# One planner for five engines: a planning delay for TensorE steps, other engines for the scaling of probabilities, and another way to turn q and k in two pairs

## The chip, the core and the metric

The kernel runs on one core of one Trainium2 chip. The core has TensorE (PE in the profile; its weight loads are the row PEld), VectorE (DVE), ScalarE (ACT) and GpSimd (POOL); SyncE (SP) issues all DMAs of this kernel. The metric is the device time of one execution in microseconds (us), median over several executions. One further execution was profiled.

## The reference

Three stages follow one another. Attention over 4 batches with 8 heads of 576 rows and 64 columns, a causal mask and a bias from a running sum; then an expert layer that takes the maximum of three products; then a second layer with a rational function.

```python
scores = scale * np.matmul(q, k.transpose(0, 1, 3, 2))
cum = np.cumsum(np.maximum(s, 0.0), axis=-1)
bias = -(cum[:, :, :, None] - cum[:, :, None, :])
scores = np.where(causal, -1000000000.0, scores + np.minimum(bias, 0.0))
attn = np.exp(scores - max);  attn = attn / (sum + 1e-09)
x = np.matmul(attn, v)                      # then 2304 tokens x 512
h = max(x @ w1, x @ w2, x @ w3);  x = h @ w_out          # d_ff 768
h = x @ w_in;  g = P(h) / Q(h);  out = g @ w_out2        # d_ff 2048
```

All products of float32 data are kept exact enough by splitting an operand into a rounded high part and the remaining low part, and adding three products.

## The kernel before, in words

**Attention.** The 32 heads are worked on in 16 pairs; pairs 0 to 3 are batch 0, and so on. For one pair:

- `load_qk` brings q and k into the tiles `raw_k` and `raw_q`. `prep_pe` (pairs 0 to 3, `pr < KM`, KM being 4) turns them by products with an identity matrix on TensorE (L401, 36 products of 64x64 in three steps: k, q and a rest `r`), copies the high part out of PSUM (L234) and subtracts for the low part on VectorE (L408). `prep` (the other pairs) turns them with VectorE's transpose instruction (L416, one for k and one for q), copies the high part on ScalarE or VectorE (L234) and subtracts on GpSimd or VectorE (L237). Its loads are eight DMAs of 140 KB in place of two of 288 KB.
- `scores` multiplies q by k and adds the bias (L450, four groups of row tiles), VectorE adds the mask and takes the row minimum (L467), ScalarE does exp and the row sum (L474).
- `norm` scales the rows by the reciprocal of their sum (L483 on GpSimd or VectorE, L481 on ScalarE), ten tiles for a pair: first tiles 2, 1, 0 of both heads, then tiles 4, 3. In pairs 0 to 3 the planner chooses between GpSimd, ScalarE and VectorE; in later pairs GpSimd does all ten.
- `flip` turns the scaled probabilities on TensorE (L515, 30 products in ten steps); ScalarE or VectorE copies them out (tile `PT`). `values` multiplies by v (L558); the result is split into `x` (L234, L570).

**First expert layer.** `experts` does one of 36 groups for a batch (12 products each, L186 with 288 columns). A group of a batch needs `x` of all four pairs of it, so TensorE has such groups to do only from the end of pair 3 on. The weights are loaded, decoded on VectorE (L594, L596, L598) and split. VectorE or ScalarE takes the result (`hs`, L674, L234).

**The rest.** When the last pair is done, its tiles are freed, and the weights of the second layer come back from DRAM (`ws`). TensorE does the remaining expert groups meanwhile, then `moe1_out`, and then the chunks of the second layer (L186 with 384 columns, L894), 96 of them.

**What sets the order.** Nothing is scheduled while the program runs: every engine works through its own list in order, and a waiting instruction holds up everything behind it. The lists come from `Plan.issue`, which runs once while the program is built. A step has engines that can do it with a cost in us on each, a rank (about the pair's number, plus a fraction for the stage), and the steps that it depends on. `est[m]` is the planned time at which step m's inputs are there: the planned end of the step before it plus a lag for the handover (`LAG`). Again and again the planner takes the step that can start first, and among those that could start on an engine at once the one of the lowest rank. A step that more than one engine could do (`anyof`) goes by planned end, weighted by `PRICE`. So a cost or a planned time that is changed alters no instruction by itself but the order on every engine, and through it the PSUM banks and the engine of the steps that have a choice.

Of the kernel before, what the change touches and what calls it, by code (L numbers as in the profile page):

```python
# [24 lines left out]
class Plan:  # L25
# [3 lines left out]

    LAG = {"pe": 0.2, "dve": 0.12, "act": 0.14, "pool": 0.09, "sp": 0.0, "ctl": 0.0}  # L30
    SAME = {"pe": 0.0, "dve": 0.11, "act": 0.1, "pool": 0.05, "sp": 0.0, "ctl": 0.0}
    BEGIN = {"dve": 0.9, "act": 2.0, "pool": 0.75, "sp": 0.75}
    AHEAD = 5.0
    TURN = 0.2
# [28 lines left out]
    def issue(self):  # L63
        steps = self.steps
        left = [len(s[3]) for s in steps]
        after = [[] for _ in steps]
        for n, s in enumerate(steps):
            for p in s[3]:
                after[p].append(n)
        end = [0.0] * len(steps)  # L70
        est = [0.0] * len(steps)
        engine = {e: self.BEGIN.get(e, 0.0) for s in steps for e in s[0]}
        ready = {e: set() for e in engine}
        for n, s in enumerate(steps):
            if not left[n]:
                for e in s[0]:
                    ready[e].add(n)
        idle = [(0.0, b) for b in self.banks]
        wire = 0.0
        mode = None  # L80
        for _ in steps:
            best = None
            for e, cand in ready.items():
                t = engine[e]
                mine = None
                for n in cand:
                    engs, rank, _, _, take, _, kb, new = steps[n]
                    start = max(t, est[n], wire - self.AHEAD if kb else 0.0)
                    if take:
                        if len(idle) < len(take):  # L90
                            continue
                        start = max(start, idle[len(take) - 1][0])
                    if len(engs) > 1 and any(max(engine[o], est[n]) + c * self.PRICE[o] < start + engs[e] * self.PRICE[e] for o, c in engs.items() if o != e):
                        continue
                    key = (max(start, t + 0.1), rank + (self.STAY if new and new != mode else 0.0), n)
                    if mine is None or key < mine[0]:
                        mine = (key, start)
                if mine is not None and (best is None or mine[1] < best[0]):
                    best = (mine[1], mine[0][2], e)
            start, n, e = best  # L100
            engs, _, fn, _, take, free, kb, new = steps[n]
            cost = engs[e]
            if new:
                cost += self.TURN if new != mode else 0.0
                mode = new
            for o in engs:
                ready[o].discard(n)
            for h in take:
                h.bank = idle.pop(0)[1]
            fn(e) if len(engs) > 1 else fn()  # L110
            engine[e] = start + cost
            if kb:
                wire = max(wire, start + cost) + kb / 190.0
                end[n] = wire + 2.0
            else:
                end[n] = start + cost
            lag = self.LAG[e]
            for h in free:
                idle.append((end[n] + lag, h.bank))
                idle.sort(key=lambda x: x[0])  # L120
            for m in after[n]:
                if "ctl" in steps[m][0]:
                    at = start
                else:
                    at = end[n] + (0.0 if kb else self.SAME[e] if list(steps[m][0]) == [e] else lag)
                est[m] = max(est[m], at)
                left[m] -= 1
                if not left[m]:
                    for o in steps[m][0]:
                        ready[o].add(m)  # L130
        return max(end)
# [3 lines left out]
def kernel(  # L135
# [25 lines left out]
    KM = DM // 128  # L161
# [32 lines left out]
    def open_pool(name, **kw):  # L194
        g = tc.tile_pool(name=name, bufs=1, reuse_waits="tile", **kw)
        open_pools[name] = g
        return g.__enter__()
# [29 lines left out]
    def anyof(engs, rank, fn, reads=(), writes=(), free=(), pre=()):  # L227

        if len(engs) == 1:
            return plan.add(engs, rank, lambda: fn(*engs), reads, writes, (), free, pre=pre)  # L230
        return plan.add(engs, rank, fn, reads, writes, (), free, pre=pre)
# [7 lines left out]
    def dm(rank, kb, out, in_, reads=(), writes=(), pre=()):  # L239
        return plan.add({"sp": 0.45}, rank, lambda: nc.sync.dma_start(  # L240
            out=out() if callable(out) else out, in_=in_() if callable(in_) else in_), reads, writes, kb=kb, pre=pre)
# [4 lines left out]
    at = open_pool("at", side="right")  # L246
# [30 lines left out]
    def smc(y, i):  # L277
        return SMC[i] + y * (3 if i < 3 else 2)
# [10 lines left out]
    def raw_of(pr, nm):  # L289

        return (RAW[pr][nm], ("x", 2 * pr - 2 + (nm == "q"))) if pr in (1, 2) else (raw[nm], ("raw", nm))
# [9 lines left out]
    def load_qk(pr, rank, pre=()):  # L301


        b, h = divmod(2 * pr, H)
        if pr < KM:
            for nm, src in (("k", k), ("q", q)):
                t, key = raw_of(pr, nm)
                dm(rank, 288, t[:, 0:S], src[b, h:h + 2].rearrange("y (p f) d -> (y p) (f d)", p=64),
                   [key], [("raw", pr, nm)], pre)
            return  # L310
        for nm, src in (("k", k), ("q", q)):
            t, key = raw_of(pr, nm)
            for y in range(2):
                x = src[b, h + y].rearrange("(p f) d -> p (f d)", p=32)
                for u in range(2):
                    dm(rank, 143, t[64 * y + 32 * u:64 * y + 32 * u + 32, 0:1120],
                       x[:, 32 * u:32 * u + 1120], [key], [("raw", pr, nm, y, u)], pre)

    def load_v(pr, rank, nj, last):
# [5 lines left out]
        if last and pr % 2 == 0:  # L325
            dm(rank, 64, VE[pr // 2 % 2][0:64], v[b, h:h + 4, 512:576].rearrange("h p d -> p h d"),
               (), [("ve", pr // 2 % 2)])

    load_qk(0, -2)

    def ones():
# [153 lines left out]
    def norm(pr, tiles, rank):  # L485
        u = pr % 2
        sm = smalls[u]
        c0, c1 = (0, 6) if 0 in tiles else (6, 10)
        keys = [("sum", u, y, i) for y in range(2) for i in tiles]

        def small():
            nc.vector.tensor_scalar(sm[:, 2, c0:c1], sm[:, 1, c0:c1], 1e-9, None, ALU.add)
            nc.vector.reciprocal(sm[:, 2, c0:c1], sm[:, 2, c0:c1])  # L493

        ve(rank, 0, small, keys, [("rc", u, c0)], cost=0.3)
        for y in range(2):
            for i in tiles:
                r0, nr = IT[i]
                t = P[y][i][0:nr, 0:r0 + nr]
                m = smc(y, i)  # L500
                n = r0 + nr
                anyof({"pool": 0.24 + 0.00084 * n, "act": 0.2 + 0.00083 * n, "dve": 0.12 + 0.00055 * n} if pr < KM else {"pool": 0.24 + 0.00084 * n}, rank + 0.02,
                      lambda e, t=t, nr=nr, m=m: scale_by(e, t, sm[0:nr, 2, m:m + 1]), [("rc", u, c0)], [("P", y, i)])

    def t_turn(pr, x):
# [178 lines left out]
    for pr in range(NP):  # L684
        if pr > 2:
            load_qk(pr, pr - 1.3)
        (prep_pe if pr < KM else prep)(pr, pr - 0.6)
        if pr > 1:
            bias_rows(pr, pr - 0.6)
        load_v(pr, pr - 0.3, 4, True)  # L690
        for g in range(4):
            scores(pr, (g,), pr + 0.1 * g)
            if g % 2:
                norm(pr, (2, 1, 0) if g == 1 else (4, 3), pr + 0.25)
        for g in range(5):
            for y in range(2):
                flip(pr, y, g, pr + 0.5 + 0.02 * g)
        new_x(pr, pr + 0.8)
        values(pr, (0, 1), pr + 0.8)
        if pr == 0:  # L700
            weights()
        if pr == 0:

            dm(0.9, 2, cf[:, 0:4], coef_a.rearrange("(o n) -> o n", o=1).to_broadcast([128, 4]), (), ["cf"])
            dm(0.9, 2, cf[:, 8:10], coef_b.rearrange("(o n) -> o n", o=1).to_broadcast([128, 2]), (), ["cf8"])
            ac(1.5, 2, coefs, ["cf8"], ["cf4"])
            ve(1.5, 2, lambda: nc.vector.memset(cf[:, 6:7], 1.0 + 1e-6), (), ["cf6"])
        if pr % KM == KM - 1:
            n0 = len(plan.steps)
            for x in range(NG):  # L710
                experts(pr // KM, x)
            late.update(range(n0, len(plan.steps)))
# [76 lines left out]
    for i, (_, kind, x) in enumerate(need[:20 + 2 * KF1]):  # L789
        rank = NP + 0.5 + 4.5 * i / 32  # L790
# [127 lines left out]
    for c in range(len(chunks) + 4):  # L918
        n, fc = chunks[min(c, len(chunks) - 1)]
# [50 lines left out]
```

## Time and profile before

| | |
|---|---|
| time, median of 3 runs | 920.23 us (918.13 to 921.01) |
| the profiled execution's own time | 920.25 us |
| its span, first to last instruction | 918.5 us |
| TensorE busy | 891.0 us, 97% of the span |
| weight loads of TensorE | 817.3 us, 89% |
| VectorE, ScalarE, GpSimd busy | 641.9, 502.1, 417.9 us |

Of the time of the profiled execution 1.75 us lie outside the span. An engine's busy time is an average over stages with different limits, and the ends of TensorE's products are modelled, so the shares of stages, and what an engine waited for there, say more than the sums.

### The profile page before, as it was taken

How to read it: one execution, taken by the hardware profiler on the slowest of the kernel's cores; microseconds unless marked ns; L12 is line 12 of the kernel's file. 1: busy time of each engine (PE TensorE's matmuls, PEld its weight loads, DVE VectorE, ACT ScalarE, POOL GpSimd, SP SyncE). 2: the span in 40 equal slices, each digit the busy share in tenths (PEclk: the TensorE clock that was granted, in tenths of full speed). 3: DMA queues.
4: the chain of work that ended last, by engine and by line, in shares of the span. 5: the costliest groups of instructions: out<-in, count | busy, mean ns of one | idle time of the engine just before them, and what ended most of it. 6: DMA issues, size and time to landing. Idle time of an engine off the chain costs nothing.

```text
span 918.5 us, 17333 instructions
## 1 busy us (share of the span) xinstructions
PE 891.0 (97%) x6224; PEld 817.3 (89%) x6224; DVE 641.9 (70%) x1423; ACT 502.1 (55%) x1200; POOL 417.9 (46%) x504
## 2 busy tenths in 40 slices
PE   6888999999999999999999999999999999999998
PEld 6777889899988999999978989998999999999997
DVE  6899988695777876231389478668838856884875
ACT  5686554463444544222476376457637646663764
POOL 3467655352233422488864254245325424541442
PEclk9999999999999999999999999999999999999999
DMA  7296756676664663564400010011001001100000
GB/s 212 63 220 163 205 163 187 195 212 194 189 196 138 195 201 119 177 202 129 146 1 1 27 60 1 1 36 52 1 26 61 1 1 51 37 0 1 35 1 35
DMA packets 71734, 90.34 MB, mean 98 GB/s; under 512 B 24864, under 2 KB 53024, under 8 KB 71616
## 3 DMA queue, kind: packets, MB, share of 16 engines
q1 hardware_dynamic: 71648, 89.23, 32.9%
q8 instruction: 49, 0.80, 0.4%
q14 instruction: 37, 0.30, 0.1%
HBM read 67.31 MB, written 21.82 MB: 97 GB/s over the span
## 4 chain that ended last, share of the span: by engine, by line
PE 85%; DVE 7%; POOL 3%; ACT 2%; issue 1%; DMA 1%; SPq 0%; POOLq 0%; DVEq 0%; ACTq 0%
PE bank L186 50%; PE bank L894 22%; PE bank L515 5%; PE bank L558 4%; PE bank L450 4%; POOL P L483 2%; DVE P L467 2%; ACT P L474 1%; PE bank L401 1%; DVE wx L596 1%; DVE wx L594 1%; DVE wx L598 0%; DMA ws<-w_dram 0%; DVE T_q L416 0%; DVE qkT L408 0%
## 5 line engine op out<-in xcount | busy, mean ns | idle before, releaser
L186 PE MATMUL bank<-x,w 128*128 128x288 f32 x1728 | 247.7, 298 | 0.0
L186 PEld LDWEIGHTS bank<-x,w 128*128 128x128 f32 x1728 | 231.6, 188 | 2.9 <-issue 1.4
L894 PE MATMUL bank<-ws,g 128*128 128x512 f32 x864 | 215.7, 394 | 2.0 <-ACT g L873 1.7
L186 PE MATMUL bank<-x,ws 128*128 128x384 f32 x1008 | 189.6, 337 | 0.0
L894 PEld LDWEIGHTS bank<-ws,g 128*128 128x128 f32 x864 | 160.8, 188 | 32.1 <-ACT g L873 2.1
L186 PEld LDWEIGHTS bank<-x,ws 128*128 128x128 f32 x1008 | 178.2, 188 | 7.4 <-ACT x L831 0.4
L483 POOL TENSOR_SCALAR P<-P,small 128x320 f32<-128x320 f32 (+4 forms) x147 | 92.3, 644 | 133.0 <-DVE small L493 119.3
L850 POOL TENSOR_SCALAR q<-a,cf 128x384 f32<-128x384 f32 x96 | 64.3, 670 | 185.5 <-ACT a L845 173.3
L474 ACT ACTIVATE P<-P,small 128x320 f32<-128x320 f32 (+4 forms) x160 | 88.4, 556 | 35.9 <-DVE small L467 35.3
L674 DVE TENSOR_TENSOR hs<-bank,hs 128x288 f32<-128x288 f32 x96 | 43.5, 453 | 83.2 <-PE bank L186 67.4
L852 POOL TENSOR_TENSOR q<-q,a 128x384 f32<-128x384 f32 x96 | 97.8, 1018 | 8.0
L234 ACT COPY PT<-bank 128x512 f32<-128x512 f32 (+4 forms) x186 | 68.3, 424 | 49.9 <-PE bank L515 43.3
L867 DVE SCALAR_TENSOR_TENSOR q<-q,cf,bank 128x384 f32<-128x384 f32 x96 | 58.7, 612 | 43.2 <-ACT bank L865 39.4
L862 ACT ACTIVATE a<-q,cf 128x384 f32<-128x384 f32 x96 | 59.2, 617 | 50.6 <-POOL q L852 50.3
L515 PE MATMUL bank<-ident,P 128*128 128x128 f32 x480 | 71.4, 281 | 14.5 <-POOL P L483 14.3
L515 PEld LDWEIGHTS bank<-ident,P 128*128 128x128 f32 x480 | 55.5, 142 | 24.7 <-POOL P L483 21.2
L186 PE MATMUL bank<-h,ws 128*128 128x384 f32 x432 | 75.9, 336 | 0.0
L853 DVE TENSOR_TENSOR t<-bank,t 128x384 f32<-128x384 f32 x96 | 52.9, 551 | 32.9 <-ACT t L847 32.9
L186 PEld LDWEIGHTS bank<-h,ws 128*128 128x128 f32 x432 | 75.0, 188 | 0.5
L873 ACT CAST g<-t 128x384 fp32r<-128x384 f32 x96 | 49.3, 513 | 45.1 <-DVE t L871 44.9
L764 POOL TENSOR_TENSOR h<-h 128x384 fp32r<-128x384 f32 x36 | 37.3, 1053 | 67.1 <-ACT h L763 67.1
L847 ACT ACTIVATE t<-bank,cf 128x384 f32<-128x384 f32 x96 | 63.9, 666 | 0.7 <-PE bank L186 0.7
(87 smaller groups left out, 1216.4 us busy)
## 6 DMA issues: line engine op xcount, KB each, us to landing
raww<-in_moe_w_out_dram SPq DMA_DIRECT2D x22, 512.0 KB, 4.1
raww<-in_moe_w_dram SPq DMA_DIRECT2D x18, 512.0 KB, 5.9
w_dram<-wx SPq DMA_DIRECT2D x36, 256.0 KB, 2.3
ws<-w_dram SPq DMA_DIRECT2D x36, 256.0 KB, 3.0
raww<-in_moe_w_in_dram SPq DMA_DIRECT2D x14, 512.0 KB, 4.4
h_dram<-hs SPq DMA_DIRECT2D x48, 144.0 KB, 2.3
h<-h_dram SPq DMA_DIRECT2D x36, 192.0 KB, 2.7
raw_k<-in_k_dram SPq DMA_DIRECT2D x48, 140.0 KB, 3.0
```

Of the source, the lines that this page charges most:

```text
L186: nc.tensor.matmul(ps, l, r, start=(i == 0), stop=(i == len(seq) - 1))
L234: nc.scalar.copy(out=out, in_=in_) if e == "act" else (nc.vector if e == "dve" else nc.gpsimd).tensor_copy(out, in_)
L474: ac(rank + 0.04, 0, lambda Pi=Pi, W=W, m=m, nr=nr: nc.scalar.activation(out=Pi[0:nr, 0:W], in_=Pi[0:nr, 0:W], func=ACTF.Exp, bias=sm[0:nr ...
L483: (nc.vector if e == "dve" else nc.gpsimd).tensor_scalar(t, t, c, 0.0, ALU.mult, ALU.add)
L515: nc.tensor.transpose(hold.bank[:, o:o + 128], P[y][i][:, 128 * j:128 * j + 128], ident)
L847: ac(rank, 0, lambda: nc.scalar.activation(out=t2[kt], in_=hold.bank[:, 0:TB], func=ACTF.Identity, scale=cf[:, 3:4], bias=cf[:, 2:3]), [(" ...
L850: po(rank, 0, lambda: nc.gpsimd.tensor_scalar(t2[kq], t2[ka], cf[:, 5:6], cf[:, 4:5], ALU.mult, ALU.add), [ka, "cf4"], [kq], cost=0.75)
L852: po(rank, 0, lambda: nc.gpsimd.tensor_tensor(t2[kq], t2[kq], t2[ka], ALU.mult), [ka], [kq], cost=0.97)
L853: ve(rank, TB, lambda: nc.vector.tensor_tensor(t2[kt], hold.bank[:, 0:TB], t2[kt], ALU.mult), [("hp", ci)], [kt])
L862: ac(rank, 0, lambda: nc.scalar.activation(out=t2[a], in_=t2[qq], func=ACTF.Ln, bias=cf[:, 6:7], scale=1.0), [kq, "cf6"], [ka], cost=0.52)
L867: ve(rank, 0, lambda: nc.vector.scalar_tensor_tensor(t2[qq], t2[qq], cf[:, 6:7], hold.bank[:, 0:TB], ALU.add, ALU.mult), [kr], [kq], cost= ...
L894: nc.tensor.matmul(hold.bank, t2[kg][:, ga, ts], w2["o2", fc][:, wb, :], start=(fc == 0 and x == 0), stop=(fc == KF2 - 1 and x == 2))
```

## The change

Three things change, all in how the program is planned or which form a step takes; the mathematics stays.

1. **A planning delay.** A step that TensorE can do, of rank above 4.0, whose input comes from another engine or a DMA, is planned to have that input 0.5 us later than before (`SLACK`). No instruction waits longer by itself; the planner prefers other work of TensorE for that half microsecond.
2. **Scaling.** Every tile's scaling may now go to GpSimd (at a planned cost raised by 0.11 us) or ScalarE, in all pairs; VectorE is no longer a choice.
3. **q and k of pairs 2 and 3.** Identity products on TensorE are left to pairs 0 and 1; pairs 2 and 3 take `prep`, with its loads.

```diff
+    SLACK = 0.5
...
-                est[m] = max(est[m], at)
+                est[m] = max(est[m], at + (self.SLACK if steps[m][1] > 4.0 and "pe" in steps[m][0] and e not in ("pe", "ctl") else 0.0))
...
-        if pr < KM:
+        if pr in (0, 1):
             for nm, src in (("k", k), ("q", q)):
...
-                anyof({"pool": 0.24 + 0.00084 * n, "act": 0.2 + 0.00083 * n, "dve": 0.12 + 0.00055 * n} if pr < KM else {"pool": 0.24 + 0.00084 * n}, rank + 0.02,
+                anyof({"pool": 0.35 + 0.00084 * n, "act": 0.2 + 0.00083 * n}, rank + 0.02,
...
-        (prep_pe if pr < KM else prep)(pr, pr - 0.6)
+        (prep_pe if pr in (0, 1) else prep)(pr, pr - 0.6)
```

Over the whole program, scalings go from 147 on GpSimd, 5 on ScalarE and 8 on VectorE to 100, 60 and 0; TensorE's identity products of `prep_pe` go from 144 to 72, VectorE's transposes from 24 to 28. Line numbers behind the first added line are one higher in the changed kernel.

Three places show what the planner makes of it. The first is TensorE's list behind the scores of pair 0; P_i are probabilities of pair 0, raw_k and raw_q belong to pair 1. Before:

```order
L450 MATMUL bank_68<-EXT_94 128x448
L515 MATMUL bank_69<-ident,P_2_98 128x128 x3
L401 MATMUL bank_70<-ident,raw_k 64x64 x16
L401 MATMUL bank_71<-ident,raw_q 64x64 x16
L515 MATMUL bank_72<-ident,P_2_103 128x128 x3
L515 MATMUL bank_73<-ident,P_1_97 128x128 x2
```

The same place in the changed kernel:

```order
L451 MATMUL bank_68<-EXT_94 128x448
L402 MATMUL bank_69<-ident,raw_k 64x64 x16
L516 MATMUL bank_70<-ident,P_2_98 128x128 x3
L516 MATMUL bank_71<-ident,P_2_103 128x128 x3
L516 MATMUL bank_72<-ident,P_1_97 128x128 x2
L516 MATMUL bank_72<-ident,P_0_96 128x128
L402 MATMUL bank_73<-ident,raw_q 64x64 x16
```

The product with raw_k now stands ahead of the first flip, which needs a scaled tile; and in the rows that follow (not shown) the first half of the scores of pair 1 stands ahead of the values of pair 0, where it stood behind them.

The second place is VectorE's list where q and k of pair 2 are turned; qkT_91 belongs to pair 1, and the rows L467 or L468 are the row minima of pair 1. Before:

```order
L408 TENSOR_TENSOR qkT_91<-bank_71,qkT_91 128x2x64
L408 TENSOR_TENSOR qkT_90<-bank_66,qkT_90 128x64x8
L594 TENSOR_SCALAR wx_117<-raww_115 128x512
L596 SCALAR_TENSOR_TENSOR wx_117<-raww_115,wx_117 128x512
L570 TENSOR_TENSOR x_130<-bank_67,x_130 128x320
L570 TENSOR_TENSOR x_130<-bank_68,x_130 128x256
L467 ISA P_2_98,small_108<-bank_69,mask 128x320
```

The same place in the changed kernel:

```order
L409 TENSOR_TENSOR qkT_91<-bank_66,qkT_91 128x2x64
L409 TENSOR_TENSOR qkT_91<-bank_73,qkT_91 128x64x8
L417 STREAM_TRANSPOSE T_k<-raw_k 128x18x32
L235 CAST qkT_90<-T_k 128x576
L417 STREAM_TRANSPOSE T_q<-raw_q 128x18x32
L468 ISA P_2_98,small_108<-bank_66,mask 128x320
```

Two transposes and a copy stand where a subtraction and the first decode of an expert weight stood; that decode moves behind the first row minima of pair 2.

The third place is ScalarE's list in pair 6, a pair whose scaling GpSimd did alone. Before (exp of tiles 0 and 4, then 3, then copies for the flips):

```order
L474 ACTIVATE P_0_101,small_107<-P_0_101,small_107 64x64
L234 CAST w_5_0_149<-wx_118 128x512
L474 ACTIVATE P_4_100,small_107<-P_4_100,small_107 128x576
L474 ACTIVATE P_4_105,small_107<-P_4_105,small_107 128x576
L474 ACTIVATE P_3_99,small_107<-P_3_99,small_107 128x448
L474 ACTIVATE P_3_104,small_107<-P_3_104,small_107 128x448
L234 COPY PT<-bank_73 128x3x128
```

The same place in the changed kernel:

```order
L475 ACTIVATE P_4_100,small_107<-P_4_100,small_107 128x576
L235 COPY hs_127<-bank_69 128x288
L475 ACTIVATE P_4_105,small_107<-P_4_105,small_107 128x576
L235 CAST qkT_90<-T_k 128x576
L482 ACTIVATE P_2_98<-P_2_98,small_107 128x320
L482 ACTIVATE P_1_97<-P_1_97,small_107 128x192
L482 ACTIVATE P_0_96<-P_0_96,small_107 64x64
L475 ACTIVATE P_3_99,small_107<-P_3_99,small_107 128x448
L475 ACTIVATE P_3_104,small_107<-P_3_104,small_107 128x448
L235 COPY PT<-bank_70 128x3x128
```

Three scalings (L482) stand between the exponentials, and a copy `hs` that needs an expert group of TensorE stands ahead of them in the same list.

## Rows read from the trace of the kernel before

**Rows 1.** Windows cut at the starts of the values of pairs 0 to 4
```profile
core 0: us, PE busy (x) PEld busy (x) DVE busy (x) ACT busy (x) POOL busy (x), PEclk, DMA share, GB/s
0.00:25.56 25.56, 18.35 (x254) 16.65 (x254) 14.96 (x46) 15.61 (x42) 9.10 (x31) 0.93 0.69 191
25.56:46.27 20.71, 18.28 (x259) 15.17 (x255) 18.80 (x65) 14.12 (x45) 10.63 (x14) 0.92 0.27 72
46.27:60.52 14.25, 12.60 (x123) 10.13 (x119) 13.38 (x42) 11.71 (x37) 9.60 (x11) 0.88 0.85 215
60.52:72.61 12.09, 10.91 (x111) 8.36 (x111) 11.99 (x40) 10.96 (x36) 8.49 (x10) 1.00 0.85 205
72.61:92.24 19.63, 17.35 (x143) 15.49 (x142) 17.78 (x32) 13.01 (x39) 13.80 (x18) 1.00 0.62 163
92.24:370.76 278.52, 271.66 (x2401) 249.70 (x2402) 210.78 (x562) 135.88 (x414) 110.80 (x142) 1.00 0.61 181
370.76:463.24 92.48, 92.43 (x657) 90.96 (x656) 27.11 (x52) 28.93 (x61) 71.71 (x69) 1.00 0.52 162
463.24:466.00 2.76, 0.77 (x3) 0.34 (x3) 2.69 (x6) 2.09 (x5) 2.14 (x3) 1.00 0.01 3
466.00:918.50 452.50, 448.67 (x2290) 410.54 (x2290) 324.36 (x583) 269.77 (x528) 181.62 (x210) 1.00 0.07 22
```
**Rows 2.** Waits of TensorE: total us, times, longest us
```profile
PE bank L515 <- POOL P L483: 14.3, 18, 2.3
PE bank L401 <- DMA raw_k<-in_k_dram: 4.7, 1, 4.7
```
**Rows 3.** TensorE in order of time: start, us, idle before and its releaser
```profile
16.85 0.73 PE L515 MATMUL bank<-ident,P 128*128 128x128 f32 x3 [1.84 <-POOL P L483]
...
24.48 1.15 PE L401 MATMUL bank<-ident,raw_q 64*64 64x64 f32 x32
25.56 2.82 PE L558 MATMUL bank<-PT,v 128*64 128x320 f32 x28
...
36.84 0.33 PE L401 MATMUL bank<-ident,raw_q 64*64 64x64 f32 x4
...
37.22 1.91 PE L515 MATMUL bank<-ident,P 128*128 128x128 f32 x9
...
111.75 0.66 PE L515 MATMUL bank<-ident,P 128*128 128x128 f32 x4 [1.38 <-POOL P L483]
```
**Rows 4.** VectorE's groups by form: count, busy us, mean ns
```profile
L416 DVE STREAM_TRANSPOSE T_k<-raw_k 128x576 f32<-128x576 f32 x12 | 15.0, 1250 | 0.0
L408 DVE TENSOR_TENSOR qkT<-bank,qkT 128x512 fp32r<-128x512 f32 x8 | 5.5, 690 | 4.9 <-ACT qkT L234 4.9
L483 DVE TENSOR_SCALAR P<-P,small 64x64 f32<-64x64 f32 x5 | 2.3, 470 | 0.0
L234 DVE COPY PT<-bank 128x384 f32<-128x384 f32 x4 | 2.2, 546 | 0.0
L596 DVE SCALAR_TENSOR_TENSOR wx<-raww,wx 128x512 uint32<-128x512 uint32 x54 | 43.3, 803 | 1.0
```
**Rows 5.** VectorE's first decode instruction: minimum, median, maximum ns; then one of them
```profile
L594 DVE TENSOR_SCALAR wx<-raww x54: 402/417/2518, 26.9 to 357.1; 128x512 uint32<-128x512 uint32 x54
78.97 2.52 DVE L594 TENSOR_SCALAR wx<-raww 128x512 uint32<-128x512 uint32 x1
```
**Rows 6.** GpSimd in order of time, around 80 us
```profile
78.39 1.44 POOL L237 TENSOR_TENSOR qkT<-T_k,qkT 128x576 fp32r<-128x576 f32 x1
79.79 1.41 POOL L237 TENSOR_TENSOR qkT<-T_q,qkT 128x576 fp32r<-128x576 f32 x1
82.68 3.40 POOL L483 TENSOR_SCALAR P<-P,small 128x576 f32<-128x576 f32 x4 [1.48 <-DVE small L493]
```
**Rows 7.** ScalarE: a scaling by form, and what its `hs` copies waited for
```profile
L481 ACT ACTIVATE P<-P,small 128x448 f32<-128x448 f32 x4 | 2.6, 678 | 0.0
ACT hs L234 <- PE bank L186: 65.1, 33, 4.4
```

## The prediction

> **What bounds the kernel now.** I read three views in this order: busy time in windows cut at the starts of the values of pairs 0 to 4, the waits of TensorE, and TensorE in order of time. The windows show where TensorE is the limit and where it isn't [rows 1]. From 466 us to the end it is idle 452.50 - 448.67 = 3.8 us, and from 370.76 to 463.24 us 0.05 us: nothing to be had there, and what comes earlier moves the whole rest earlier. Just before 466 us it lacks 2.0 us. From 92.24 to 370.76 us (pairs 4 to 15, expert groups between) it is idle 278.52 - 271.66 = 6.86 us. The first 92.24 us are the loose part: idle 7.21 + 2.43 + 1.65 + 1.18 + 2.28 = 14.75 us, of which 4.74 are the wait for the first load [rows 2]. The granted clock was 0.93, 0.92 and 0.88 in the first three windows and 1.00 behind, so that TensorE stood at the lower of its two levels (1.2 and 2.4 GHz) for part of it; against a full clock that is 0.07 x 25.56 + 0.08 x 20.71 + 0.12 x 14.25 = 5.2 us.
>
> In that part another engine is nearly full: from 25.56 to 92.24 us VectorE is busy 18.80 + 13.38 + 11.99 + 17.78 = 61.95 of 66.68 us, 93% [rows 1]; ScalarE 49.8, 75%, but 10.96 of 12.09 in one window. So there the end is set by chains through VectorE, ScalarE and GpSimd, not by TensorE alone. Its waits are nearly all of one sort: a flip waits for a tile scaled on GpSimd, 18 times, 14.3 us [rows 2].
>
> **Part 1, identity products of pairs 2 and 3.** Removed from TensorE: for one pair two steps of sixteen products and one of four. One of the large ones takes 25.56 - 24.48 = 1.08 us to the next step, the rest step 37.22 - 36.84 = 0.38 us [rows 3]. So 2 x (2 x 1.08 + 0.38) = 5.1 us at the full clock, all before 92 us.
>
> VectorE gives up four subtractions of 0.69 us, 2.8 us, and takes four transposes of 1.25 us, 5.0 us [rows 4]. ScalarE's casts are about even (two large ones of a pair stay, the small one goes). GpSimd gets four subtractions of 1.42 us [rows 6], 5.7 us; it is busy 42.5 of the 66.7 us [rows 1], so they fit. On SP's queue two loads become eight for each of the two pairs; the first expert weights are queued behind them. Four transfers of 288 KB become sixteen of 140 KB (sizes in the section on the kernel), 1.15 against 2.24 MB: at the 191 GB/s of the first window about 5.7 us of transfer. The next window moves only 72 GB/s, so there is room, and the decode that needs the weight is planned later anyway (second place shown). I cost that at nothing; without the room it would be those 5.7 us once, on the weights, which nobody needs before the end of pair 3.
>
> **Part 2, scaling.** Of the eight scalings that leave VectorE I count the five small ones, 2.3 us; three of four wide copies leave it too (one 384-column copy remains), 3 x 0.546 = 1.6 us [rows 4]. Before the values of pair 4 two weight decodes fewer stand in VectorE's list, 9 for 11: about 0.42 + 0.80 + 0.80 = 2.0 us each [rows 4, 5], 4.0 us that move behind 92 us, where VectorE is busy 210.78 of 278.52 us, 76% [rows 1]. VectorE's sum up to pair 4: -2.8 + 5.0 - 2.3 - 1.6 - 4.0 = -5.7 us.
>
> In pairs 4 to 15 ScalarE takes part of what GpSimd did alone. Tiles 4 and 3 of both heads cost GpSimd 3.40 us in a row [rows 6]; with the two 448-column tiles on ScalarE at 0.68 us each [rows 7], beside GpSimd's two others, the last tile is ready after some 1.8 us, 1.6 us earlier. Twelve of the 18 waits lie behind 92 us, the longest 1.38 us [rows 3], and they make up nearly all of that window's 6.86 us. ScalarE has the time: 135.88 of 278.52 us busy.
>
> **Part 3, the planning delay.** It adds no instruction. Its worth is that TensorE does an expert group first where it would have stood at a flip; its cost could be a flip that comes later than it could. Expert groups suffice: 105 are done at the end of pair 15 in both orders, so the 39 left over, and the 92 us in which the weights of the second layer come back, stay as they are.
>
> **The sum.** Start to the values of pair 4: 5.1 us of products go. The product that now precedes the first flip covers its 1.84 us wait [rows 3], and scores of pair 1 ahead of the values of pair 0 start pair 1's chain earlier. VectorE permits it: 5.7 us of work less, and 66.68 - 61.95 = 4.7 us idle. I take 5.1 + 1.84 = 7 us. Ends: nothing if another chain holds the same pace, 14.75 - 4.74 + 5.2 = 15 us if every wait and the slow clock go. Pairs 4 to 15: of 6.86 us I take 5, as the twelve waits are shorter than the 1.6 us saved and the planner adds half a microsecond; the ends are 6.86 and a loss, below. The 2.0 us before 466 us stay. Together 12 us: span 918.5 - 12 = 906.5, and with the 1.75 us outside 908 us. The profiled execution took 920.25 us, the median of the runs shown is 920.23, so nothing has to be corrected.
>
> **Rivals.** *More.* TensorE alone sets the pace of the first pairs: the 10 us of idle time and half of the slow clock go, 12.6, and all 6.86 behind: 19.5 us, 901 us. For it: of those 10 us some 14.3 - 6.8 = 7.5 are flips that wait for a scaling [rows 1, 2]. Against it: VectorE at 93%.
>
> *Given back on VectorE.* VectorE's first decode instruction usually takes 0.417 us; one that started at 78.97 us took 2.52, and over just that time GpSimd ran two of the very subtractions that are to be four more, until 81.20 us [rows 5, 6]. If each of the four holds up a VectorE instruction for its length, 5.7 us come back, VectorE's saving is zero, and the first part gains 1.3 us: 6.3 in all, 914 us. Against it: the mean transposes in this trace take 1.25 us, and only the decode shows such outliers. The Trainium skill (SBUF — State Buffer, "SBUF: two separate sides") has a rule for it: VectorE and GpSimd share a pair of ports that one of them holds for a whole instruction, while the other stops; the 2.52 us agree with it. By that rule the change moves work the wrong way (more on GpSimd while VectorE is nearly full) and the time is this rival's; by the windows alone GpSimd's extra work is free and the time is the forecast.
>
> *Slower: ScalarE's list holds the scaling.* ScalarE's copies `hs` wait for an expert group, 33 times, 65.1 us in all, 2.0 us each [rows 7], and at present nobody suffers. In the changed list such copies stand ahead of scalings (third place shown). A scaling that sits behind one is late, and the flip that needs it stops TensorE. Twelve pairs have two sets of scalings each, 24 places; at 2.0 us less the half microsecond of delay a place costs 1.5 us. From 8 places on the gain of 12 is gone; at 12, half of them, it is 18 - 12 = 6 us slower, 926 us. Against it: the expert group of such a copy stands ahead of those flips in TensorE's list too, so it is mostly done by then.
>
> *It doesn't do what it says.* TensorE's waits only change their name (the same flips wait for ScalarE or for VectorE's row minima), and the 5.1 us of products end in a longer wait for pair 1: 920 us. Against it: those products stood in windows where TensorE was busy 88 to 90% of the time.
>
> **Chances.** Forecast 0.45, with its own range of 903 to 914; more 0.15; given back on VectorE 0.20; no effect 0.08; slower 0.12. A measurement of this kernel can't tell less than 0.3% from no change, 917.5 to 923 us here. Faster: the first three but for 0.01 of the third, 0.79. Same: 0.08 and that 0.01, 0.09. Slower 0.12. The range of 899 to 919 us leaves out the slower case, most of no effect and a little below: 2 in 10.
>
> **What would show it.** In the profile after: the values of pair 4 start at about 85 us; fewer L401 products, and a granted clock nearer to 1.00 in the first 60 us; waits of flips for a scaling well below 14.3 us in all, below 3 from pair 4 on; the last values some 12 us earlier, and a stretch behind them that is as long as before. The forecast is wrong if TensorE's waits name L481's successor on ScalarE for more than a few us, if decode instructions of 1 to 2.5 us multiply before pair 4, or if TensorE waits for expert weights.

## The result, and the profile after

The changed kernel takes 907.93 us (median of 4 runs, 907.28 to 908.80) against 919.88 us before (918.13 to 921.01): ratio 0.9872, 95% interval 0.9853 to 0.9892, so 1.3% faster. The forecast was 908.0 us. A second set of runs of the same two programs gave 908.43 against 918.83 us, 0.9883 [0.9866, 0.9900]. The profiled execution took 908.51 us with a span of 906.7 us.

So the sum came out. Its two terms did not: the first part gained about 4 us where 7 were forecast, the main part 7.7 where 5 were. That these two errors cancel is luck. This is the view of the windows after, cut at the starts of the values of pairs 0 to 4 and 15 and at the first output products of the second expert layer; it answers to [rows 1], with the same columns.

```profile
core 0: us, PE busy (x) PEld busy (x) DVE busy (x) ACT busy (x) POOL busy (x), PEclk, DMA share, GB/s
0.00:27.79 27.79, 18.25 (x255) 16.55 (x255) 16.56 (x49) 16.79 (x44) 10.64 (x33) 0.88 0.79 191
27.79:43.90 16.11, 13.15 (x128) 9.90 (x127) 15.64 (x59) 15.56 (x53) 7.54 (x10) 0.97 0.49 134
43.90:55.10 11.20, 10.91 (x104) 8.29 (x103) 11.10 (x29) 9.28 (x28) 9.74 (x12) 0.89 0.78 210
55.10:71.32 16.22, 12.76 (x111) 9.85 (x111) 16.12 (x49) 13.70 (x45) 13.52 (x15) 0.89 0.72 186
71.32:88.27 16.95, 16.74 (x147) 15.12 (x146) 15.76 (x34) 14.42 (x43) 12.00 (x13) 1.00 0.55 160
88.27:359.05 270.78, 269.30 (x2396) 251.91 (x2395) 205.92 (x552) 154.77 (x455) 92.08 (x106) 1.00 0.63 188
359.05:454.40 95.35, 93.26 (x660) 91.36 (x659) 29.34 (x56) 31.67 (x66) 73.91 (x72) 1.00 0.50 158
454.40:906.70 452.30, 448.53 (x2290) 410.42 (x2290) 321.65 (x583) 272.87 (x528) 184.03 (x210) 1.00 0.07 22
```

Read it against [rows 1] stage by stage. The values of pair 4 start 92.24 - 88.27 = 3.97 us earlier. From there to the values of pair 15 the kernel takes 270.78 us for 278.52, 7.74 less. The next stretch takes 0.11 us more, the last 0.20 less. Together 3.97 + 7.74 - 0.11 + 0.20 = 11.8 us, the difference of the two spans.

In the first 88.27 us TensorE is busy 71.81 us instead of 77.49 (5.7 less; the identity products are 5.1 of them by the forecast's price, and one expert group fewer but a third of a pair's scores more stand ahead of pair 4), but idle 16.46 us instead of 14.75: part of what the products gave was spent waiting. VectorE is busy 15.64 + 11.10 + 16.12 + 15.76 = 58.6 of 60.5 us from pair 0 to pair 4, 97% where it had been 93%. From pair 4 to 15 TensorE is idle 1.48 us instead of 6.86.

The waits of TensorE (total us, times, longest us):

```profile
PE bank L402 <- DMA raw_k<-in_k_dram: 4.4, 1, 4.4
PE bank L402 <- POOL P L348: 4.3, 1, 4.3
PE bank L516 <- POOL P L484: 3.2, 5, 1.3
PE bank L451 <- DVE small L468: 2.3, 2, 1.4
PE bank L516 <- ACT P L482: 1.9, 1, 1.9
```

Flips (L516) wait 3.2 + 1.9 us for a scaled tile where it had been 14.3 us in 18 waits [rows 2]. Two kinds are new: 4.4 us for a load in front of an identity product (the other 4.3 are the kernel's first load, as before), and 2.3 us for VectorE's row minima (`small`). TensorE in order of time shows where:

```profile
17.45 1.97 PE L402 MATMUL bank<-ident,raw_k 64*64 64x64 f32 x32 [4.37 <-DMA raw_k<-in_k_dram]
19.36 2.18 PE L516 MATMUL bank<-ident,P 128*128 128x128 f32 x9
...
25.50 0.71 PE L451 MATMUL bank<-qkT 64*128 64x320 f32 x6
...
27.79 2.82 PE L559 MATMUL bank<-PT,v 128*64 128x320 f32 x28
...
176.85 0.66 PE L516 MATMUL bank<-ident,P 128*128 128x128 f32 x4 [0.65 <-POOL P L484]
```

The k product of pair 1 starts at 17.45 us, and the first flips behind it. Before, the first flip started at 16.85 us after its 1.84 us wait [rows 3]. The product didn't cover a wait; it brought a longer one. Its load was issued at 10.20 us in both kernels; it landed at 16.36 us before, half a microsecond ahead of the first flip, and at 17.32 us after, where more loads follow it on the queue. TensorE's idle time up to the values of pair 0 grew from 7.21 to 9.54 us, and they came at 27.79 us instead of 25.56. 32 of the 48 products of pair 1's scores are done by then, from 25.50 us on; before, all of them came behind those values, from 28.43 us on. Behind pair 4 one flip waits for a scaling, 0.65 us, where the longest of twelve had been 1.38.

VectorE in order of time shows what stood in front of the exponentials of pair 1:

```profile
23.29 0.39 DVE L235 CAST qkT<-bank 128x128 fp32r<-128x128 f32 x1 [2.51 <-PE bank L402]
23.71 0.99 DVE L409 TENSOR_TENSOR qkT<-bank,qkT 128x128 fp32r<-128x128 f32 x2
24.62 1.25 DVE L417 STREAM_TRANSPOSE T_k<-raw_k 128x576 f32<-128x576 f32 x1
25.91 0.46 DVE L235 CAST qkT<-T_k 128x576 fp32r<-128x576 f32 x1
26.28 1.25 DVE L417 STREAM_TRANSPOSE T_q<-raw_q 128x576 f32<-128x576 f32 x1
27.38 0.48 DVE L468 CUSTOM_DVE_ANT_0 P<-bank,mask 128x320 f32<-128x320 f32 x1
```

VectorE waits 2.51 us for the identity products of pair 1, which the late load pushed back. From then on it works without a gap, and the two transposes and the copy of pair 2 (24.62 to 27.53 us) stand ahead of the row minima of pair 1 (L468). The exponentials of pair 1 follow at 28.30 us (30.44 before). The view of the chain that ended last names a load of q, issued at 23.00 us, in front of the second transpose; that load is pair 3's and landed at 27.12 us, after the transpose had begun. The four loads of q that this transpose needs had landed by 22.99 us. So what stands on the path here is pair 1's load and VectorE's new work, not the new loads themselves.

These rows answer to the rivals: VectorE's first decode instruction (minimum, median, maximum ns); its third decode instruction up to the values of pair 4, before and after; what ScalarE's `hs` copies waited for; and the scalings on ScalarE by form.

```profile
L595 DVE TENSOR_SCALAR wx<-raww x54: 392/418/1644, 38.5 to 348.2; 128x512 uint32<-128x512 uint32 x54
```
```profile
L598 DVE SCALAR_TENSOR_TENSOR wx<-raww,wx x10: 658/679/1119, 32.5 to 89.8; 128x512 uint32<-128x512 uint32 x10
```
```profile
L599 DVE SCALAR_TENSOR_TENSOR wx<-raww,wx x8: 677/1038/1802, 43.6 to 86.2; 128x512 uint32<-128x512 uint32 x8
```
```profile
ACT hs L235 <- PE bank L187: 65.0, 31, 4.4
```
```profile
L482 ACT ACTIVATE P<-P,small 128x448 f32<-128x448 f32 x20 | 13.4, 673 | 2.0 <-DVE small L494 2.0
```

The median of the first decode stays at 418 ns, and the longest is 1.64 us where it had been 2.52 [rows 5]. But the third decode became slower, its median up to pair 4 from 679 to 1038 ns. Counted over all VectorE instructions up to pair 4 that ran more than 0.15 us longer than the median of their kind in the kernel before, the surplus is 7.9 us in 13 instructions before and 10.1 us in 17 after, 10.2 in the second execution; each of the 13 and of the 17 ran beside an instruction of GpSimd. So VectorE was held up, and by 2.2 us more than before. The `hs` copies wait as long as before [rows 7], yet TensorE waited for a scaling on ScalarE once, 1.9 us.

### The profile page after: what moved, and what is told of

Same layout as the page of the kernel before. It is cut to its first block, busy times and chain, and to the rows that moved or that the text cites. A ratio compares the mean times of both kernels' runs of the same rounds, so it can differ in the third digit from the quotient of the medians.

```text
span 906.7 us, 17047 instructions
## 1 busy us (share of the span) xinstructions
PE 882.9 (97%) x6080; PEld 813.4 (90%) x6080; DVE 632.1 (70%) x1403; ACT 529.1 (58%) x1257; POOL 403.4 (44%) x467
## 4 chain that ended last, share of the span: by engine, by line
PE 88%; DVE 4%; DMA 3%; ACT 2%; POOL 1%; issue 1%; SPq 1%; DVEq 0%; POOLq 0%; ACTq 0%
PE bank L187 53%; PE bank L895 22%; PE bank L516 4%; PE bank L451 4%; PE bank L559 4%; DMA raw_q<-in_q_dram 2%; SPq L241 1%; ACT P L475 1%; DVE P L468 1%; DVE T_q L417 1%; POOL ws L238 0%; DVE wx L595 0%; DVE wx L599 0%; POOL P L484 0%; DVE T_k L417 0%
## 5 line engine op out<-in xcount | busy, mean ns | idle before, releaser
L851 POOL TENSOR_SCALAR q<-a,cf 128x384 f32<-128x384 f32 x96 | 66.8, 696 | 183.6 <-ACT a L846 175.0
L484 POOL TENSOR_SCALAR P<-P,small 128x320 f32<-128x320 f32 (+4 forms) x100 | 63.3, 651 | 151.3 <-DVE small L494 109.4
L516 PE MATMUL bank<-ident,P 128*128 128x128 f32 x480 | 70.3, 282 | 5.4 <-POOL P L484 3.2
L846 ACT ACTIVATE a<-bank 128x384 f32<-128x384 f32 x96 | 46.9, 489 | 39.2 <-PE bank L187 38.7
L468 DVE CUSTOM_DVE_ANT_0 P<-bank,mask 128x320 f32<-128x320 f32 (+4 forms) x160 | 62.0, 420 | 10.4 <-PE bank L451 7.0
```

The costliest lines, as they stand in the source:

```text
L468: nc.vector.tensor_tensor_reduce(Pi[0:nr, j0:j1], hold[y].bank[0:nr, at0:at0 + j1 - j0], mask[0:nr, m0:m0 + j1 - j0], -scale, sm[0:nr, 3, ...
L484: (nc.vector if e == "dve" else nc.gpsimd).tensor_scalar(t, t, c, 0.0, ALU.mult, ALU.add)
L516: nc.tensor.transpose(hold.bank[:, o:o + 128], P[y][i][:, 128 * j:128 * j + 128], ident)
L851: po(rank, 0, lambda: nc.gpsimd.tensor_scalar(t2[kq], t2[ka], cf[:, 5:6], cf[:, 4:5], ALU.mult, ALU.add), [ka, "cf4"], [kq], cost=0.75)
```

## Experiments

Twelve runs follow, one of them the changed kernel again; each is compared with the kernel before on its own chip. Two questions were put. Which part brings the gain behind pair 4: the delay, by letting TensorE do other work first, or the scaling, by having the tile earlier? And what sets the pace before pair 4: TensorE, so that products taken away are a gain, or the chains through VectorE, ScalarE and the loads, so that they are not? "V4" is the start of the values of pair 4, "main" the stretch from there to the values of pair 15. Shifts of stages come from one profile each and are corrected for the expert groups and scores that a kernel's order puts into another stage (1.66 us a group and 3.56 us a pair's scores, from the rows); the changed kernel's are -3.5 and -8.2 us.

**One part at a time.** The delay alone:

```
+    SLACK = 0.5
...
-                est[m] = max(est[m], at)
+                est[m] = max(est[m], at + (self.SLACK if steps[m][1] > 4.0 and "pe" in steps[m][0] and e not in ("pe", "ctl") else 0.0))
```

> The planning delay alone. Theory L (the waits of flips went because scaling on two engines ends sooner): the delay alone leaves the chain of scaling on GpSimd as long as it was; TensorE's waits for L484 from pair 4 on fall a little, from 6.8 to about 5 us, and the time to about 918 us (0.2%). Rival D (the waits went because the planner puts expert groups ahead of flips): those waits fall to 2 us or less with GpSimd still doing all scaling of later pairs, and the time falls to about 914 us (0.6%).

Measured 914.63 us, 0.9943 [0.9931, 0.9955]: the time of rival D. The scaling alone (the `anyof` line, on GpSimd or ScalarE for every pair):

> The scaling on GpSimd or ScalarE alone. Theory L: the waits from pair 4 on fall to 2 us or less, VectorE loses its eight scalings, and the time falls by 5 to 7 us to about 914 (0.6 to 0.7%). Rival D: the waits stay at 5 us or more, gain of 2 us at most, 918 us.

Measured 914.68 us, 0.9955 [0.9938, 0.9971]: the time of theory L. Transposes instead of identity products for pairs 2 and 3 alone (twice `if pr in (0, 1)` for `if pr < KM`):

> VectorE's transposes for pairs 2 and 3 alone. Theory P (5.1 us of products leave TensorE at a place where it is part of the limit): the values of pair 4 start some 4 us earlier, 916 us (0.45%). Rival Q (pairs 0 to 3 are set by loads, VectorE and ScalarE, and the sixteen loads push the first chain back by what the products gave): the values of pair 4 start within 1.5 us of 92.2, and the time is within 0.2% of before.

Measured 922.53 us, 1.0025 [1.0014, 1.0036]; the values of pair 4 start at 91.60 us. That is rival Q, and a little worse. Delay and scaling without the transposes:

> The changed kernel with identity products kept for pairs 2 and 3 (delay and scaling together). Theory L and P, parts adding up: the stretch of pairs 4 to 15 is as short as in the changed kernel (some 271 us), the first part is 3 to 4 us longer than there, time about 911 to 912 us (0.9%). Rival Q: the same time as the changed kernel, 908 us, or better.

Measured 912.89 us, 0.9921 [0.9907, 0.9936], main -6.7 us, and V4 3.0 us later than in the changed kernel: the parts add up, as the first theory had it. The main stretch of the first three, with the columns of the windows; first the delay, then the scaling, then the transposes:

```profile
90.31:362.24 271.93, 267.97 (x2388) 248.31 (x2387) 215.40 (x562) 136.80 (x415) 111.90 (x142) 1.00 0.63 187
```
```profile
89.02:361.67 272.65, 270.03 (x2396) 251.75 (x2395) 204.23 (x545) 155.78 (x456) 91.73 (x102) 1.00 0.62 184
```
```profile
91.60:371.42 279.82, 270.78 (x2395) 251.75 (x2395) 213.77 (x546) 142.23 (x417) 111.84 (x147) 1.00 0.61 181
```

TensorE's idle time is 3.96, 2.62 and 9.04 us there, 6.86 before. What flips waited for GpSimd in that stretch, before, with the delay and with the scaling:

```profile
PE bank L515 <- POOL P L483: 6.8, 12, 1.4
```
```profile
PE bank L516 <- POOL P L484: 3.8, 4, 1.9
```
```profile
PE bank L515 <- POOL P L483: 1.8, 4, 0.7
```

With the delay the waits lie between the two theories, 3.8 us for 5 and 2; with the scaling they are 1.8 us, and 0.7 more for ScalarE. The delay does it with GpSimd as busy as ever (111.90 us), by doing other work first; the scaling by taking 19 us off GpSimd. They are two cures of the same waits: alone they are worth 5.2 and 4.1 us of 920 by their ratios, together 7.3, not 9.4. The transposes alone are worth nothing; they lose 0.25%.

**Two parts at a time, and the whole again.** The changed kernel itself, beside the next three on one chip:

> The changed kernel again, on the chip and in the rounds of the next three: 0.987 of before, 908 us. If the first stretch is set by TensorE's granted clock, which differs between executions, the values of pair 0 start some 2 us earlier or later than 27.8 us with a higher or lower clock in that window, with the same list of instructions.

Measured 0.9883, as told above. The values of pair 0 start at 27.73 us, with the same granted clock of 0.88 in that window, so this run doesn't test the clock; other runs do, as the last section tells. Delay and transposes:

> Planning delay and transposes for pairs 2 and 3, scaling as before. Theory P (the products are worth 4 to 5 us as soon as the later pairs no longer wait for the scaling): 5.4 us for the delay and 4.5 for the products, about 910 us (0.989). Rival I (what the transposes are worth is a chance of the order that the planner ends with): within 2 us of the delay alone, 914 to 916 us, as the transposes alone gave +2.4 us.

Measured 912.99 us, 0.9935 [0.9922, 0.9948]: beside the delay alone the transposes are worth nothing that can be told. Scaling and transposes:

> Scaling and transposes, no planning delay. Theory P: 4 to 5 us for each, about 911 us (0.990). Rival I: within 2 us of the scaling alone, 914 to 916 us.

Measured 909.96 us, 0.9899 [0.9884, 0.9915], which is 0.56% better than the scaling alone. So by the timed ratios the transposes pay beside the new scaling and not without it. The profiles show the same for V4, if kernels are put together whose engines have the same lists up to about 67 us (the delay changes nothing before):

| lists up to about 67 us | shift of V4, us, one profile each |
|---|---|
| as before | 0 (before), -1.9 (delay) |
| transposes | -0.2 (alone), -1.5 (with the delay), -1.5 (and the scaling of pairs 4 to 15, below) |
| scaling | -2.7 (alone), -0.5 (with the delay) |
| both | -3.5 (no delay), -3.5 and -3.5 (changed kernel), -4.7 (delay of 1.0 us, below), -3.9 (scaling of pairs 0 to 3 only, below) |

One and the same list spans some 2 us, so neither part by itself is shown to move V4; both together do.

**Which scaling lets them pay.** Transposes with the new choice of engine for pairs 0 to 3 only, or for the pairs from 4 on only; the line of the first:

```
+ anyof({"pool": 0.35 + 0.00084 * n, "act": 0.2 + 0.00083 * n} if pr < KM else {"pool": 0.24 + 0.00084 * n}, rank + 0.02,
```

> Transposes for pairs 2 and 3, and the new choice of engines for scaling in pairs 0 to 3 only (later pairs on GpSimd as before, no delay). The transposes alone gave 1.0025, with the new scaling everywhere 0.990. Theory E (VectorE, which takes the transposes, must not scale as well; the interaction lies in the first pairs): 0.994 or lower, 914 us. Rival T (it lies in the later pairs, where GpSimd alone is late): 1.000 or higher, 919 us.

Measured 913.85 us, 0.9927 [0.9912, 0.9942]; V4 -3.9 us, main -3.9.

> Transposes for pairs 2 and 3, and the new choice for scaling in pairs 4 to 15 only (pairs 0 to 3 may still scale on VectorE). Theory E: 0.998, no more than the scaling alone gave. Rival T: 0.992 or lower, 911 us.

Measured 914.88 us, 0.9936 [0.9919, 0.9953]; V4 -1.5 us, main -6.8. The first figure of theory E came true, its second (0.998) didn't, and rival T missed with 1.000: each half of the scaling brings 0.9 to 1.0% beside the transposes, and both halves together 1.3%. The later half gains in its own stretch. The early half gains as much behind pair 4, where its choice of engines is the old one, as before it; no theory expected that, and I can't say which change of order did it.

**The load in front of the first wait.** If the k product of pair 1 waits for its load, an earlier load should bring pair 0 forward. Pair 1's loads no longer wait for an earlier one:

```
-        load_qk(pr, -2 + pr, [last])
+        load_qk(pr, -2 + pr, [last] if pr == 2 else ())
```

> The changed kernel with the loads of pair 1 free to start before the running sum is done (they waited for it). The first k product of pair 1 waited 4.4 us for its load. If that wait sets the values of pair 0 and all behind (theory W), they start 3 to 4 us earlier and the time falls to about 904 us. Rival V: another chain (exp and scaling of pair 0, VectorE) sets them, the wait moves to the first flip, and the time changes by less than 1.5 us.

Measured 909.86 us, 0.9905 [0.9891, 0.9919]: no gain over the changed kernel (0.9883 on the same chip). Its waits of TensorE:

```profile
PE bank L516 <- ACT P L482: 7.8, 3, 4.1
PE bank L516 <- POOL P L484: 6.1, 9, 1.4
PE bank L402 <- DMA raw_k<-in_k_dram: 4.5, 1, 4.5
```

The 4.5 us left are the kernel's first load. The other wait for a load is gone, and its length stands at a flip that waits for ScalarE's scaling, 4.1 us in one piece. The values of pair 0 start at 26.63 us, 1.2 earlier, but those of pair 4 at 90.41, 2.1 later, with one expert group more ahead of them. The two chains end nearly together; shortening one shows the other. In the second profile of the changed kernel the same 4.7 us wait is even put down to VectorE's `small` instead of the load, though the load landed there at 17.66 us and the product began at 17.79.

**One more pair off TensorE.** Identity products for pair 0 alone (`if pr == 0` in both places), pair 1 by transposes. By the forecast's price this takes away another 2.5 us:

> The changed kernel with identity products for pair 0 only; pair 1 is turned on VectorE and its loads become eight. Theory P (products off TensorE are worth some 2.5 us a pair): 905 to 906 us. Rival B (before pair 4 VectorE and the loads set the pace, so what TensorE saves is lost there): 908 to 912 us, and the values of pair 4 start no earlier than 88 us.

Measured 913.45 us, 0.9917 [0.9903, 0.9931]: 0.3 to 0.45% slower than the changed kernel (0.9883 and 0.9872), 3 to 4 us. What its flips waited for:

```profile
PE bank L516 <- POOL P L484: 15.0, 12, 2.4
```

By that price TensorE has 2.5 us less to do, and its flips wait 15.0 us for GpSimd instead of 3.2. V4 moved by -1.2 us (-3.5 in the changed kernel), main by -5.6 (-8.2): the loss is in both, in the profile of the slowest of its six executions. Its granted clock was 0.83, 0.85 and 0.79 in the first three windows, the lowest of these kernels taken together, so slower products are part of the loss; whether the longer waits brought the clock down is not shown. Before pair 4 a product taken from TensorE is not time taken from the kernel, and the new order that comes with it is worse behind pair 4 as well.

**A longer delay.** `SLACK = 1.0`:

> The changed kernel with a planning delay of 1.0 us for 0.5. The delay gave 5 us alone and 1 to 2 us on top of the other two parts. Theory L (what is left of the waits is short, and 0.5 us covers it): within 0.3% of the changed kernel, 907 to 910 us. Rival D (longer is better): the few waits of flips from pair 4 on go altogether, 905 us.

Measured 907.31 us, 0.9854 [0.9837, 0.9870]. The main stretch:

```profile
90.52:355.19 264.67, 264.30 (x2348) 247.15 (x2346) 202.12 (x540) 158.43 (x466) 89.89 (x96) 1.00 0.64 191
```

Idle 0.37 us: nothing is left there for a delay to gain. The waits of flips from pair 4 on are gone, as rival D had it, but the time is theory L's. Its interval overlaps the changed kernel's; it is at best a little faster, and was the fastest that ran.

## Why the prediction was right, point by point

- **Start to V4, 7 us forecast, 4.0 measured: mis-sized.** Two steps failed. "The product that now precedes the first flip covers its 1.84 us wait": there was nothing to cover, as the product's own load landed only half a microsecond before that flip could start; now the product waits 4.37 us for it. And "VectorE permits it: 5.7 us of work less": it was 1.7, as the next point tells, and the transposes stand ahead of pair 1's row minima in VectorE's list. "I cost that at nothing", for the loads, held for the weights; but the load of pair 1 landed 0.4 to 1.3 us later in three executions of the new order, with more loads behind it. The step "5.1 us of products go" holds as a sum of busy time but not as a gain: alone, the transposes brought nothing, and they gained only beside the new scaling. The forecast had that scaling as a permission; the runs bear this out, but not which of its effects gives it.
- **VectorE's list, 5.7 us less forecast: right in sign, mis-sized.** Up to the values of pair 4 its work is 75.2 us where it had been 76.9, 1.7 less. The copies of the turned q and k, counted as even on ScalarE, came to VectorE: five of 3.9 us up to there in place of three of 1.6. Of the wide copies of `PT` one left before pair 4, not three. And its long instructions cost 2.2 us more. From pair 0 to pair 4 it is busy 58.6 us where it had been 61.9, but in a stretch shorter by 6.2 us, so fuller than before. To the lower end named, "another chain holds the same pace", the kernel with identity products for pair 0 only comes nearest, with V4 -1.2 us.
- **Pairs 4 to 15, 5 us forecast, 7.7 measured: mis-sized.** The idle time fell by 5.4 us, near the 5 forecast. The other 2.4 came out of TensorE's *busy* time. Most of that stands at the flips: the 330 of the stretch took 48.90 us before and 47.20 after. The waits of the weight loads suggest why; over the whole program the same flips stood there as (before, then after)

```profile
PEld bank L515 <- POOL P L483: 21.2, 26, 2.7
```
```profile
PEld bank L516 <- POOL P L484: 5.4, 8, 1.5
```

  21.2 us in 26 waits against 14.3 in the row of the matmuls [rows 2]: 0.27 us a wait in which the load of the next weights didn't run beside a matmul, and the matmuls behind it took longer. In this stretch alone the waits of the weight loads, of all kinds, fell from 19.6 to 8.4 us, 11.2 less, more than the stretch gained; in every one of the runs its corrected gain lies between the fall of the matmuls' idle time and the fall of these waits. This is worked out from the rows; no run tested it by itself. The end "6.86" was no bound.
- **Delay and scaling.** The forecast gave both one term and did not price them apart; alone they give 0.57 and 0.45%, together 0.79.
- **The 2.0 us before 466 us and the rest: right.** TensorE still waits there for `g`, in all 2.1 us, and the stretch behind is 452.30 us for 452.50.
- **The clock nearer to 1.00 in the first 60 us: wrong.** 0.88, 0.97, 0.89 and 0.89 in the first four windows, no better than before.
- **The rivals.** *Slower* did not come: the `hs` copies wait 65.0 us as before, and from pair 4 on no flip waited for a scaling on ScalarE. *Given back on VectorE* came in part. The rule of the Trainium skill (SBUF — State Buffer, "SBUF: two separate sides") that for some VectorE instructions one of GpSimd and VectorE holds a shared pair of ports for a whole instruction, while the other stops, would have cost 5.7 us by the reading of this rival. The trace agrees with the rule in kind, as all long VectorE instructions before pair 4 ran beside GpSimd; the surplus grew by 2.2 us. But not through the four subtractions: with transposes alone the surplus is 7.1 us, with the scaling alone 9.8 (8.0 and 10.1 with the delay beside them), and 7.9 before. Nor does "only the decode shows such outliers" hold for the kernel before: its copies of T_q took 0.42 to 1.68 us. *More* failed in the first part and came near in the main one, 7.7 us for 6.86. *It doesn't do what it says* was half true in the first part: the waits did change their name there.

What stays open: why the transposes alone are slower, 0.25%, though V4 didn't move (their main stretch has 9.04 us idle, flips wait 15.9 us for GpSimd; and 1.5 of the 2.7 us by which the profiled execution is longer stand behind the first output product of the second layer, where its granted clock fell, as the last section tells), why they pay beside the new scaling, and the 3.9 us that the scaling of pairs 0 to 3 brought behind pair 4.

## What to carry to other kernels

Where several engines are over 90% full, price work taken from one of them only after finding which chain ends last there, and trace every input of the instructions that take its place, their loads first, and every engine that gets the work, its copies too: here 5.1 us of removed products brought nothing alone, and 2.5 us less to do made the kernel 3 to 4 us slower. In a stretch where TensorE is the limit, a wait costs more than the idle time of its matmul row; here it cost less than that of the weight-load row. Two edits that cure the same waits don't add up: run each alone.

## What the runs showed of the hardware that I had not expected

The kernel before and the kernel with the delay alone have the same instructions in the same order on every engine up to about 76 us, behind the values of pair 3. Yet the values of pair 0 started at 25.56 us in one execution and at 23.11 in the other, with TensorE busy 18.35 and 14.96 us for 254 and 255 matmuls. The first window of the delay alone:

```profile
0.00:23.11 23.11, 14.96 (x255) 13.55 (x255) 14.88 (x46) 15.68 (x42) 9.11 (x31) 1.00 0.76 211
```

The granted clock is 1.00 where it was 0.93 in [rows 1]. The scaling alone and the scaling with the delay are another such pair: 26.75 us at 1.00 and 29.30 us at 0.83. A single profile of the first part is therefore good to about 2 us, and the shifts of V4 above should be read so; the timed ratios carry the verdicts.

The same shows at the wait of about 2 us before the first output product of the second layer. Two executions of the changed kernel, 456 to 462 us, the one shown above first:

```profile
456.00:462.00 6.00, 6.00 (x31) 5.20 (x30) 6.00 (x13) 5.58 (x12) 3.38 (x4) 1.00 0.00 0
```
```profile
456.00:462.00 6.00, 6.00 (x25) 5.15 (x24) 6.00 (x13) 5.68 (x12) 3.56 (x5) 0.77 0.00 0
```

After a wait of 1.8 us the clock stayed at 1.00, after one of 2.1 us it was 0.77, and 25 matmuls ran in the time of 31; the stretch behind took 452.30 and 453.93 us. But behind the 2.0 us idle of the kernel before it stayed at 1.00 and took 452.50 us [rows 1], so the length alone doesn't decide. Such a wait can cost 1.6 us more than itself in one execution and not in the next. The fourteen profiles part in two halves here. In seven the granted clock was 1.00 in the 8 us behind the first output product, and from that product on the program took 453.3 to 453.5 us; in the other seven it was 0.79 and the time 454.7 to 455.5 us, so TensorE stood at the lower of its two levels for part of those 8 us. The waits before were 1.7 to 2.1 us in the first seven, 1.8 to 2.2 us in the others.

The long VectorE instructions are of a few kinds. In the changed kernel 35 of the 54 third decodes ran beside no GpSimd instruction, each in 666 to 695 ns; the longest of the other 19 took 1802 ns. The addition in front of the reciprocal (`small`, L493) took 155 to 173 ns alone and up to 1231 ns beside GpSimd. The transposes took 1221 to 1262 ns in either case.
